# A table of steps in another order: blocks 2 to 8 of an attention and MoE kernel

## Chip, cores and metric

The kernel runs on one core of a Trainium2 chip. The metric is the time of one execution on the device in microseconds (us). Engines: PE multiplies matrices, DVE works on vectors, ACT on scalars and activations, POOL (GpSimd) issues most loads and stores here, SP issues the DMA transposes.

## What is computed

Eight batches (B), eight heads, 576 positions (S), head dimension 64. A linear attention without softmax is normed per head and position, and feeds a two-layer perceptron over 4608 tokens:

```python
kv = np.einsum('bhsd,bhse->bhde', k, v)
out = np.einsum('bhsd,bhde->bhse', q, kv)
rms = np.sqrt(np.mean(out * out, axis=-1, keepdims=True) + 1e-06)
x = (out / rms * g_norm).transpose(0, 2, 1, 3).reshape(4608, 512)
h = x @ w_in                                    # 512 -> 2048
g = np.maximum(h, 0.0) + alpha * np.minimum(h, 0.0)
y = g @ w_out                                   # 2048 -> 512, float32
```

## The kernel before

**Tiling.** The tokens are cut into nine blocks w = 0 to 8 of 512, each of four row tiles of 128. Blocks 0 and 1 are written out directly (the loop for block 1 is `loop_one`; its 16 units u take their PSUM banks h0, h1, h2 in turn, so that the last unit has h1). For blocks 2 to 8 the functions `put_m1`, `put_m2`, `put_moves`, `put_attention` and `put_rest` register *steps*, each with a name and the names that it needs. A string ORDER (L1856 on) lists all 1085 steps, and this generator emits them:

```python
def in_order():                                                     # L1960
    todo = {".".join(map(str, s[0])): s for s in steps if s[1]}
    names, done, gates = {s[0] for s in steps if s[1]}, set(), {"-": gt_last[0]}
    for x in ORDER:
        name, _, at = x.partition("@")
        s = todo.pop(name)
        assert all(n in done or n not in names for n in s[3]), name
        if at:
            load_gate[:] = [gates[at]] if at != "!" else []
        yield s[2]
        done.add(s[0])
        gates[name] = gt_last[0]
```

Each step's instructions go to the end of its engine's queue, and each engine works through its queue in order. So ORDER fixes for every engine what stands behind what; semaphores between engines follow from the data and from the tiles in PSUM and SBUF.

**The steps.** A name is a letter, the block, and numbers.

- First product, h = x w_in: `M.w.u` (L695, four matmuls 128x512; `M.w.0` and `Ma.w.0` split them into 128 and 384 columns, L728), `r.w.u` (ACT, relu of −h out of PSUM, L704), `s.w.u` (DVE, the PReLU sum into gt, L710). In blocks 3 to 8 twelve of the 16 units are instead made by three groups s = 1 to 3 of seven products (a Strassen-like scheme): `f.w.s.1` to `f.w.s.7` are eight or four 128x256 matmuls each (L1296), `seed`, `u2`, `u3` ACT copies (L1312, L1315), `c22`, `c12` DVE sums (L1318, tile mh), `r..` and `s..` the relu and PReLU sums (L1356, L1363). `t.` and `a.` are DVE sums of x and of weights.
- Second product, y = g w_out, by the same kind of scheme: `S.` are DVE sums of gt (L864 to L886), `p.w.n.k` groups of four 128x256 matmuls (L948), `y.w.seed`, `u2`, `u3` copies (L969, L996, L998), `y.w.c11`, `c21` (ACT, L1004) and `c12`, `c22` (DVE, L1010) the finished parts, `st.` their stores (L752).
- Attention: `ld.` are loads on POOL; with `@step` a one-element copy on POOL (L1478) that reads a result of that step holds the load back, `@!` is without such a gate. `q.b.t` is a DMA transpose of q by SP (L405), `kv.b` and `kvc.b` the product k^T v and its copies. `R.w.i` (i = 1 or 3) multiplies q with kv for two row tiles, i − 1 and i, in one tile or_ps over two PSUM banks, which the next R takes again (L575, 24 or 16 matmuls of 64x64). For each of the two row tiles follow `q2` and `q3` (ACT, four squares each with a sum, L635), `rs` (ACT, the reciprocal root, L645), `n` (DVE, the norm into x_rows, L661) and `x` (a DMA transpose by SP into xt, L673), which M and f of that block read. A *group* below is R with these steps; "group 3.2" or "at 8.3" names the pair of row tiles 2 and 3 of block 3 or 8.

The squares and the norm read the same tile or_ps for their own halves:

```python
nc.scalar.activation(                                               # L635, squares
    out=sq[:, half, j], in_=o_ps[:, half, j], func=AF.Square,
    accum_out=ssq[:, half, j : j + 1],
)
nc.vector.tensor_tensor(                                            # L661, norm
    out=xr[:].rearrange("p j h d -> p h j d"), in0=o_ps,
    in1=rstd[:].unsqueeze(3).to_broadcast([P, 2, NPAIR, D]), op=ALU.mult,
)
```

The first units M.w.0 to M.w.3 have fixed PSUM banks: u = 0 has h2, u = 1 has h1, u = 2 has m0, u = 3 has m1. The list of what a step needs names the steps of blocks 2 to 8 only; for the first use of a bank after `loop_one` it names nothing, and the semaphores alone hold the order there.

Of the kernel before, what the change touches and what calls it, by code (L numbers as in the profile page):

```python
# [17 lines left out]
def kernel(  # L18
# [13 lines left out]
    B, H, S, D = q.shape  # L32
# [1819 lines left out]
    for w in range(1, NW):  # L1852
# [4 lines left out]
        M.2.2 Ma.2.0 r.2.2 S.1.1.0 M.2.0 a.2.2 M.2.1 S.1.1.1 r.2.0 s.2.2 y.1.seed M.2.3 q.3.0  # L1857
        S.1.2.1 r.2.1 s.2.0 M.2.6 s.2.1 q.3.4 kv.3 S.1.1.2 S.1.2.0 p.1.2.3 a.1.3 q.3.1 kvc.3 M.2.4
        ld.k.4.1@- S.1.1.3 S.1.4.1 p.1.6.0 S.1.2.3 r.2.3 q.3.3 S.1.2.2 p.1.6.1 r.2.4 p.1.6.2 y.1.c11
        s.2.4 p.1.6.3 q.3.2 M.2.5 a.1.1 y.1.u2 s.2.3 p.1.7.0 r.2.5 M.2.7 ld.k.4.0@s.2.3 r.2.6 s.2.5  # L1860
        R.3.1 r.2.7 p.1.7.1 q2.3.1 ld.v.4.0@s.2.5 s.2.7 p.1.7.2 p.1.7.3 q2.3.0 s.2.6 M.2.8 S.2.3.0
        y.1.u3 ld.q.4.0@s.2.6 M.2.10 q3.3.0 ld.q.4.1@s.2.3 q3.3.1 M.2.9 ld.v.4.1@- rs.3.0 p.1.4.0
        rs.3.1 n.3.0 r.2.8 p.1.4.1 r.2.10 n.3.1 p.1.4.2 p.1.4.3 r.2.9 S.2.3.1 x.3.1 R.3.3 y.1.c21
        a.1.2 M.2.11 q2.3.2 a.1.4 s.2.8 x.3.0 p.1.5.0 q2.3.3 p.1.5.1 s.2.10 M.2.12 q3.3.2 s.2.9
        p.2.1.0 S.1.4.2 rs.3.2 p.1.5.2 q3.3.3 n.3.2 p.1.5.3 S.1.4.0 p.2.1.1 x.3.2 rs.3.3 r.2.11
        M.2.14 n.3.3 r.2.12 s.2.11 R.4.1 x.3.3 p.2.1.2 y.1.c22 q2.4.0 p.2.1.3 S.2.1.0 p.1.3.0 r.2.14
        q.4.2 M.2.13 y.2.p1 s.2.14 q2.4.1 p.2.2.0 S.1.4.3 q.4.0 s.2.12 M.2.15 q3.4.1 S.2.2.0 p.1.3.1
        q.4.3 r.2.15 p.2.2.1 q3.4.0 s.2.15 p.1.3.2 p.1.3.3 q.4.1 rs.4.1 ld.q.4.4@s.2.15 Ma.3.0
        rs.4.0 y.1.c12 r.2.13 M.3.0 n.4.0 ld.q.5.4@! M.3.2 r.3.0 s.2.13 y.2.seed x.4.0 M.3.3 r.3.2
        n.4.1 p.2.6.0 S.2.1.1 r.3.3 x.4.1 kv.4 s.3.0 M.3.1 t.3.1 kvc.4 ld.v.5.1@! S.2.2.1 f.3.1.1  # L1870
        s.3.2 r.3.1 p.2.6.1 t.3.2 p.2.6.2 f.3.1.seed st.1.c21 s.3.3 R.4.3 f.3.1.6 s.3.1 q2.4.3 q.5.4
        p.2.6.3 ld.q.5.0@s.3.0 t.3.3 f.3.1.2 f.3.1.u2 S.2.4.0 f.3.1.5 ld.q.5.1@s.3.2 y.2.u2 S.2.4.1
        f.3.1.7 f.3.1.r11 f.3.2.1 st.1.c11 t.3.4 f.3.1.u3 a.2.4 p.2.7.0 q2.4.2 f.3.1.c22 f.3.1.4
        p.2.7.1 f.3.1.s11 q3.4.3 f.3.1.3 p.2.7.2 f.3.1.r22 ld.v.5.0@! f.3.1.c12 p.2.7.3 rs.4.3
        p.2.2.2 f.3.2.seed n.4.3 p.2.2.3 y.2.u3 f.3.1.s22 f.3.2.6 x.4.3 f.3.1.r12 p.2.4.0 a.3.4
        f.3.2.u2 f.3.2.2 S.3.3.0 f.3.1.r21 f.3.2.7 f.3.1.s12 q3.4.2 p.2.4.1 f.3.2.5 f.3.1.s21
        f.3.2.u3 p.2.4.2 rs.4.2 p.2.4.3 f.3.2.r11 f.3.2.c22 f.3.3.1 y.2.c21 n.4.2 f.3.2.3 f.3.2.r22
        f.3.2.4 x.4.2 f.3.2.c12 y.2.c11 R.5.1 f.3.2.s22 p.2.5.0 f.3.3.seed p.2.5.1 f.3.2.r12 q.5.2
        f.3.2.s11 p.2.5.2 ld.k.5.0@f.3.2.s22 f.3.2.r21 f.3.3.6 f.3.2.s21 p.2.5.3 q.5.3 f.3.3.u2
# [124 lines left out]
```

## Time and profile before

| what | value |
|---|---|
| median of three runs | 271.4 us (270.56, 271.40, 271.46) |
| the profiled execution | 270.63 us |
| its span, first to last instruction | 268.8 us |
| ordered part (first M.2 to last matmul) | 66.6 to 264.7 us |
| busy PE / DVE / ACT | 259.5 / 234.4 / 201.8 us |

How to read it: the page gives the busy time of each engine and the chain of work that ended last. A row of the timeline has the start, the length, the engine, the line and operation, the tiles (out<-in), the shapes, how many instructions were joined (x4), and in brackets how long the engine had been idle before it and what released it. Matmuls are pipelined and their ends are modelled, so two rows of PE overlap; the time of a group is the distance from its start to the next start. "sq_sb" is the tile of the squares, "h_ps" that of M, "yX", "yY", "yZ" those of p, "mX", "mY", "mV" those of f.

### The profile page before, as it was taken

Reading aid. Unit: us, or ns where it says so; the run is one execution under the profiler, and the core shown is the slowest. Engines: PE = TensorE matmul, PEld = TensorE weight load, DVE = VectorE, ACT = ScalarE, POOL = GpSimd, SP = SyncE. Lnnn points to the kernel's source line nnn. Section 1 sums busy time; section 2 is a strip of 40 time slices with the busy share of each in tenths; the row PEclk is TensorE's granted clock in tenths of the full one; section 3 lists DMA queues with packets and bytes.
Section 4 is the critical chain, followed back from the end, with each engine's and each line's share of the span. In section 5 each row is a group of like instructions: output and inputs, shape, how many; then the busy total and the mean of one; then the engine's idle time right before and its main releaser. Section 6 shows DMA issues by size and latency. Waiting matters only on the chain.

```text
span 268.8 us, 7233 instructions
## 1 busy us (share of the span) xinstructions
PE 259.5 (97%) x2709; PEld 189.8 (71%) x2709; DVE 234.4 (87%) x474; ACT 201.8 (75%) x707; POOL 86.3 (32%) x150
## 2 busy tenths in 40 slices
PE   5999999999998999999999999999999989999993
PEld 2554454456565668887888688878886878788883
DVE  6459956899967889999999989999899899998982
ACT  2567637786688889988999799989998986568300
POOL 8853552554152039227012080520030005201400
PEclk9999999999999999999999999999999999999998
DMA  7999999998989899898968987998230314400423
GB/s 195 190 202 206 196 198 189 174 245 171 124 123 158 137 110 149 141 144 181 146 91 128 146 181 83 146 194 120 43 101 0 101 39 127 130 0 2 118 80 118
DMA packets 65032, 35.80 MB, mean 133 GB/s; under 512 B 37396, under 2 KB 63012, under 8 KB 64996
## 3 DMA queue, kind: packets, MB, share of 16 engines
q0 software_dynamic: 31792, 24.47, 58.9%
q1 hardware_dynamic: 32500, 10.11, 22.5%
q10 hardware_dynamic: 704, 0.75, 0.9%
q8 instruction: 21, 0.34, 0.5%
q14 instruction: 15, 0.12, 0.2%
HBM read 36.71 MB, written 9.44 MB: 172 GB/s over the span
## 4 chain that ended last, share of the span: by engine, by line
PE 85%; ACT 5%; DMA 4%; DVE 3%; issue 1%; SPq 1%; DVEq 0%
PE h_ps L695 19%; PE yY L948 13%; PE mY L1296 11%; PE yX L948 10%; PE yZ L948 9%; PE y L740 5%; PE mV L1296 5%; PE mX L1296 3%; ACT sq_sb L635 3%; DMA qt_sb<-qst 3%; PE h_ps L728 2%; PE or_ps L575 2%; DMA y_sb<-in_g_norm_dram 2%; PE kv_ps L1407 1%; PE ssq_ps L500 1%; ACT m_sb L1356 1%
## 5 line engine op out<-in xcount | busy, mean ns | idle before, releaser
L695 PE MATMUL h_ps<-xt,w_in_sb 128*128 128x512 f16 x252 | 60.4, 379 | 0.0
L710 DVE SCALAR_TENSOR_TENSOR gt<-m_sb,beta_sb,h_ps 128x512 f16<-128x512 f32 x72 | 51.8, 740 | 5.1 <-ACT m_sb L704 4.4
L704 ACT ACTIVATE m_sb<-h_ps 128x512 f32<-128x512 f32 x72 | 42.1, 604 | 15.6 <-PE h_ps L695 10.8
L948 PEld LDWEIGHTS <-s 128*128 128x128 f16 x496 | 47.7, 98 | 7.5 <-issue 0.2
L635 ACT ACTIVATE sq_sb<-or_ps 128x64 f16<-128x64 f32 x192 | 41.3, 271 | 2.7 <-PE or_ps L575 2.3
L948 PEld LDWEIGHTS <-gt 128*128 128x128 f16 x384 | 37.1, 98 | 7.8 <-issue 0.4
L695 PEld LDWEIGHTS <-w_in_sb 128*128 128x128 f16 x252 | 24.2, 98 | 23.2 <-issue 0.3
L635 ACT ACTIVATION_READ_ACCUMULATOR sq_sb<-or_ps 128x1 f32 x192 | 40.5, 256 | 0.0
L752 POOL DMA_DIRECT2D out_dram<-y_sb x37 | 21.5, 587 | 49.9 <-ACT y_sb L1004 43.6
L948 PE MATMUL yX<-w_out_sb,gt 128*128 128x256 f16 x256 | 36.6, 273 | 0.0
L948 PE MATMUL yY<-wsum,s 128*128 128x256 f16 x256 | 34.5, 273 | 0.0
L1363 DVE SCALAR_TENSOR_TENSOR gt<-m_sb,beta_sb,mh 128x256 f16<-128x256 f32 x72 | 31.1, 476 | 1.2 <-ACT m_sb L1356 1.2
L1356 ACT ACTIVATE m_sb<-mh 128x512 f32<-128x512 f32 x36 | 23.9, 664 | 3.0 <-DVE mh L1318 3.0
L1318 DVE TENSOR_TENSOR mh<-mV,mu 128x512 f32<-128x512 f32 x36 | 24.6, 684 | 1.5 <-PE mV L1296 0.8
L1315 ACT COPY mu<-mY 128x512 f32<-128x512 f32 x36 | 21.7, 602 | 3.7 <-PE mY L1296 3.6
L1296 PEld LDWEIGHTS <-w_in_sb 128*128 128x128 f16 x216 | 21.0, 98 | 3.6
L661 DVE TENSOR_TENSOR x_rows<-or_ps,rstd_r 128x512 f16<-128x512 f32 x27 | 18.1, 683 | 5.5 <-ACT sq_sb L635 2.7
L1478 POOL COPY gate_sb<-gt 1x1 f16<-1x1 f16 x17 | 5.4, 320 | 41.7 <-DVE gt L710 22.9
L948 PE MATMUL yY<-wsum,gt 128*128 128x256 f16 x128 | 16.7, 272 | 0.2 <-ACT u L996 0.2
L740 PE MATMUL y<-w_out_sb,gt 128*128 128x512 f16 x64 | 16.3, 380 | 0.0
L948 PE MATMUL yZ<-wsum,s 128*128 128x256 f16 x120 | 16.3, 273 | 0.0
L948 PE MATMUL yZ<-w_out_sb,s 128*128 128x256 f16 x120 | 16.2, 272 | 0.0
(161 smaller groups left out, 471.7 us busy)
## 6 DMA issues: line engine op xcount, KB each, us to landing
kst<-in_k_dram POOLq DMA_DIRECT2D x10, 288.0 KB, 5.3
vst<-in_v_dram POOLq DMA_DIRECT2D x10, 288.0 KB, 5.8
qst<-in_q_dram POOLq DMA_DIRECT2D x10, 256.0 KB, 5.7
out_dram<-y_sb POOLq DMA_DIRECT2D x18, 128.0 KB, 4.5
w_out_sb<-in_moe_w_out_dram POOLq DMA_DIRECT2D x8, 256.0 KB, 12.3
out_dram<-y_sb POOLq DMA_DIRECT2D x7, 256.0 KB, 4.0
out_dram<-y_sb SPq DMA_DIRECT2D x5, 256.0 KB, 2.4
w_in_sb<-in_moe_w_in_dram POOLq DMA_DIRECT2D x2, 512.0 KB, 10.0
```

What stands on the lines that cost most here:

```text
L635: nc.scalar.activation(out=sq[:, half, j], in_=o_ps[:, half, j], func=AF.Square, accum_out=ssq[:, half, j : j + 1],)
L695: nc.tensor.matmul(out=h_ps[:], lhsT=w_in_blk(c, g), rhs=xts[w][:, c, :], start=(c == 0), stop=(c == NC - 1),)
L704: nc.scalar.activation(out=neg[w, g][:], in_=h_ps[:], func=AF.Relu, scale=-1.0)
L710: nc.vector.scalar_tensor_tensor(out=gts[w, i][:, r, :], in0=neg.pop((w, g))[:], scalar=beta_sb[:, g : g + 1], in1=h_ps[:], op0=ALU.mult, ...
L740: nc.tensor.matmul(out=y[:], lhsT=gt_cols(w, g, a * P, (a + 1) * P), rhs=w_out_blk(g), start=(n == 1), stop=(n == NF),)
L752: engs[store_turn[0] % len(engs)].dma_start(out=dst, in_=src)
L948: nc.tensor.matmul(out=bank, lhsT=lhs, rhs=rhs, start=fresh, stop=(c == NK - 1), skip_group_check=True,)
L1296: nc.tensor.matmul(out=t[bank][:, r, :], lhsT=lhs[:, c, r * P : (r + 1) * P], rhs=rhs[:, c, :], start=(fresh and c == r == 0), stop=(c == ...
L1315: nc.scalar.copy(out=t[what][:], in_=t["Y"][:])
L1318: nc.vector.tensor_add(out=h_tile(t, what)[:], in0=src[:], in1=u[:])
L1356: nc.scalar.activation(out=dst, in_=h, func=AF.Relu, scale=-1.0)
L1363: nc.vector.scalar_tensor_tensor(out=gts[w, i][:, r, cols], in0=m, scalar=beta_sb[:, g : g + 1], in1=h, op0=ALU.mult, op1=ALU.add,)
```

## The change

The string ORDER is another permutation of the same 1085 steps (some loads have another gate); nothing else is changed. PE has the same 2709 matmuls. The difference has 99 lines of names on each side. These hold the first step and R.3.3, ahead of which the groups p.2.1.0 and p.2.1.1 now stand (before, they stood behind it):

```diff
-        M.2.2 Ma.2.0 r.2.2 S.1.1.0 M.2.0 a.2.2 M.2.1 S.1.1.1 r.2.0 s.2.2 y.1.seed M.2.3 q.3.0
...
-        rs.3.1 n.3.0 r.2.8 p.1.4.1 r.2.10 n.3.1 p.1.4.2 p.1.4.3 r.2.9 S.2.3.1 x.3.1 R.3.3 y.1.c21
...
-        p.2.1.0 S.1.4.2 rs.3.2 p.1.5.2 q3.3.3 n.3.2 p.1.5.3 S.1.4.0 p.2.1.1 x.3.2 rs.3.3 r.2.11
...
+        M.2.1 M.2.3 r.2.1 S.1.1.1 S.1.1.2 M.2.2 r.2.3 S.1.2.2 S.1.1.0 y.1.seed Ma.2.0 S.1.2.1
...
+        p.1.6.1 S.1.2.3 s.2.3 p.2.1.0 p.1.6.2 q.3.4 a.1.1 ld.v.4.0@s.2.3 M.2.4 S.1.4.3 s.2.2 M.2.5
...
+        p.1.4.3 R.3.3 s.2.9 y.1.c21 M.2.11 q2.3.2 x.3.0 s.2.10 p.1.5.0 q2.3.3 s.2.8 p.1.5.1 S.1.4.1
```

**PE where the ordered part begins.** The rows of PE from the last group of block 1 on; w_in_sb_166 and w_in_sb_157 are the weights of two units. Before, M.2.2 is first (bank m0) and Ma.2.0 next:

```order
L948 MATMUL yX<-w_out_sb_188,gt 128x256
L695 LDWEIGHTS w_in_sb_166 [waits DMAHW3_49,DMAHW2_49,DMAHW1_49]
L695 MATMUL h_ps<-xt,w_in_sb_166 128x512 [waits PE_49]
L695 LDWEIGHTS w_in_sb_166
L695 MATMUL h_ps<-xt,w_in_sb_166 128x512
```

Now, M.2.1 (bank h1) is first:

```order
L948 MATMUL yX<-w_out_sb_188,gt 128x256
L695 LDWEIGHTS w_in_sb_157 [waits DMAHW3_49,DMAHW2_49,DMAHW1_49]
L695 MATMUL h_ps<-xt,w_in_sb_157 128x512 [waits DVE_49]
L695 LDWEIGHTS w_in_sb_157
L695 MATMUL h_ps<-xt,w_in_sb_157 128x512
```

The first matmul waits for DVE now, before for PE's own earlier one.

**ACT at group 8.3.** or_ps is the group's tile. Before, its squares stand in four pieces of four; the rows from the second piece on, of which the last waits for DVE (the norm n.8.3):

```order
L635 ACTIVATE sq_sb,ssq_r<-or_ps 128x64 x4
L996 COPY u_4044<-yY 128x512 [waits PE_49]
L645 ACTIVATE rstd_r<-ssq_r,eps_t 128x8 [waits Activation_49]
L1356 ACTIVATE m_sb<-mh 128x512 [waits DVE_49]
L1312 COPY mX<-mY 128x512 [waits DVE_49]
L1356 ACTIVATE m_sb<-mY 128x512 [waits PE_49]
L635 ACTIVATE sq_sb,ssq_r<-or_ps 128x64 x4
L1315 COPY mu_4098<-mY 128x512 [waits PE_49]
L996 COPY u_4106<-yY 128x512 [waits PE_49]
L1356 ACTIVATE m_sb<-mh 128x512
L1315 COPY mu_4123<-mY 128x512 [waits PE_49]
L635 ACTIVATE sq_sb,ssq_r<-or_ps 128x64 [waits DVE_49]
```

Now they stand in two pieces of eight (the first is split in the list by its wait), all ahead of the group's first reciprocal root:

```order
L635 ACTIVATE sq_sb,ssq_r<-or_ps 128x64 [waits PE_49]
L635 ACTIVATE sq_sb,ssq_r<-or_ps 128x64 x7
L1315 COPY mu_4014<-mY 128x512 [waits PE_49]
L1356 ACTIVATE m_sb<-mX 128x512 [waits Activation_49]
L635 ACTIVATE sq_sb,ssq_r<-or_ps 128x64 x8
L996 COPY u_4060<-yY 128x512 [waits PE_49]
L645 ACTIVATE rstd_r<-ssq_r,eps_t 128x8 [waits Activation_49]
```

No square of this group waits for a norm any more, and copies stand behind eight squares instead of four.

**POOL around the q transposes of block 4.** Its queue of DMAs (L212, L229 loads of q, L202 of k and v, L752 stores). qsb_135 is ld.q.4.4, the four 64x256 pieces are st.1.c11, the 64x2x256 pieces st.1.c21. Before:

```order
L229 DMA qsb_135<-in_q_dram 64x8x64 [waits DMAHW5_49]
L229 DMA qsb_132<-in_q_dram 64x8x64 [waits DMAHW7_49,DMASW2_49]
L202 DMA vst<-in_v_dram 128x2x576 [waits DMASW3_49,DMASW0_49,PE_49]
L752 DMA out_dram<-y_sb 64x2x256 [waits DMASW4_49,Activation_49]
L752 DMA out_dram<-y_sb 64x2x256 [waits DMASW5_49]
L1478 COPY gate_sb<-gt 1x1 [waits DVE_49,Pool_49]
L212 DMA qst<-in_q_dram 128x4x256 [waits DMAHW2_49,DMAHW0_49,DMASW6_49]
L1478 COPY gate_sb<-gt 1x1 [waits DVE_49,Pool_49]
L212 DMA qst<-in_q_dram 128x4x256 [waits DMAHW7_49,DMAHW1_49,DMASW7_49]
L752 DMA out_dram<-y_sb 64x256
```

Now:

```order
L229 DMA qsb_135<-in_q_dram 64x8x64 [waits DMAHW5_49]
L752 DMA out_dram<-y_sb 64x256 [waits DMASW2_49,Activation_49]
L752 DMA out_dram<-y_sb 64x256 [waits DMASW3_49]
L752 DMA out_dram<-y_sb 64x256 [waits DMASW4_49]
L752 DMA out_dram<-y_sb 64x256 [waits DMASW5_49]
L1478 COPY gate_sb<-gt 1x1 [waits Pool_49]
L212 DMA qst<-in_q_dram 128x4x256 [waits DMAHW7_49,DMAHW0_49,DMASW6_49]
L1478 COPY gate_sb<-gt 1x1 [waits Pool_49]
L212 DMA qst<-in_q_dram 128x4x256 [waits DMAHW1_49,DMAHW2_49,DMASW7_49,DMASW0_49]
L229 DMA qsb_132<-in_q_dram 64x8x64
L752 DMA out_dram<-y_sb 64x2x256 [waits DMASW1_49,Activation_49]
```

The store st.1.c11 moved from behind the first loads of block 5 to directly behind ld.q.4.4, and the load of v.5.1 went out of this stretch.

More of the change, by code (lines that the diff above doesn't have):

```diff
@@ L1868 @@
[L1868 to L1879, printed above, removed]
@@ new lines @@
+        p.7.4.2 f.8.3.seed p.7.4.3 f.8.2.r12 f.8.2.s22 f.8.3.6 y.7.c21 f.8.3.2 f.8.2.s21 f.8.3.u2
+        p.7.5.0 f.8.3.r11 f.8.2.s12 p.7.5.1 p.8.1.1 f.8.3.s11 f.8.3.7 f.8.3.5 S.8.1.0 f.8.3.u3
+        p.7.5.2 f.8.3.c22 p.7.5.3 f.8.3.4 S.8.2.0 f.8.3.3 f.8.3.r21 y.7.c22 p.8.1.2 p.8.6.0
+        f.8.3.c12 st.7.c22 p.8.6.1 f.8.3.s21 f.8.3.r12 p.8.1.3 f.8.3.r22 p.7.3.0 f.8.3.s12 p.7.3.1
+        y.8.p1 st.7.c21 f.8.3.s22 p.7.3.2 p.8.2.0 p.8.2.1 S.8.1.1 p.8.2.2 S.8.2.1 p.8.2.3 p.7.3.3
+        y.8.c11 p.8.6.2 y.7.c12 p.8.6.3 p.8.5.0 st.7.c12 y.8.u2 p.8.5.1 S.8.4.0 p.8.7.0 p.8.7.1
```

174 lines of the change are left out of this document (90 added, 84 removed).

## The prediction, made before the changed kernel had run

> **What bounds the kernel now.** The page's first part and the slices come first: which engine is nearest to full, and is it slowed.
>
> ```profile
> span 268.8 us, 7233 instructions
> PE 259.5 (97%) x2709; PEld 189.8 (71%) x2709; DVE 234.4 (87%) x474; ACT 201.8 (75%) x707; POOL 86.3 (32%) x150
> PEclk9999999999999999999999999999999999999998
> ```
>
> PE's matmuls set the time, at nine tenths of the clock or more in every slice. The profiled execution took 270.63 us, so 1.8 us lie around its span. The change leaves all 2709 matmuls in place, so the sum is about PE's gaps. Next come the windows by stage; after each comma stand the busy times of PE, weight loads, DVE, ACT and POOL, then clock, DMA share and GB/s.
>
> ```profile
> 66.60:97.00 30.40, 29.27 (x314) 19.05 (x313) 24.09 (x46) 24.30 (x128) 7.64 (x18) 1.00 1.00 129
> 97.00:123.00 26.00, 26.00 (x315) 21.38 (x313) 25.43 (x53) 24.09 (x102) 11.70 (x19) 1.00 0.98 143
> 174.00:204.00 30.00, 29.82 (x356) 24.57 (x354) 29.05 (x61) 27.14 (x115) 4.73 (x8) 1.00 0.62 107
> 204.00:228.00 24.00, 23.20 (x215) 19.32 (x214) 22.92 (x47) 20.23 (x65) 3.15 (x6) 1.00 0.25 71
> ```
>
> From 97 to 123 us PE has no idle time, with DVE at 98% and ACT at 93% beside it. Nothing can be won in such a stage, and a late turn of DVE or ACT costs PE at once. The other three windows miss 1.13, 0.18 and 0.80 us. A matmul's end is modelled, so I measure gaps from start to start. The pitch comes from PE's timeline where it runs freely:
>
> ```profile
> 65.75 1.04 PE L948 MATMUL yX<-w_out_sb,gt 128*128 128x256 f16 x8
> 66.62 1.03 PE L695 MATMUL h_ps<-xt,w_in_sb 128*128 128x512 f16 x4
> 67.49 1.04 PE L728 MATMUL h_ps<-xt,w_in_sb 128*128 128x384 f16 x8
> ...
> 101.06 1.04 PE L948 MATMUL yY<-wsum,s 128*128 128x256 f16 x8
> 102.02 0.41 PE L575 MATMUL or_ps<-kv_masked,qt_sb 64*128 64x64 f16 x16
> ```
>
> Four 128x512 or eight 128x256 matmuls take 0.87 us, four of the latter 0.44. Ahead of a 64x64 group stand 0.96 − 0.87 = 0.09 us more, the same in both orders. In this way I went through all starts from 66.6 us on; four places are left:
>
> ```profile
> 83.15 0.29 PE L575 MATMUL or_ps<-kv_masked,qt_sb 64*128 64x64 f16 x8
> 84.42 0.29 PE L575 MATMUL or_ps<-kv_masked,qt_sb 64*128 64x64 f16 x8 [0.98 <-DMA qt_sb<-qst]
> 84.65 1.04 PE L695 MATMUL h_ps<-xt,w_in_sb 128*128 128x512 f16 x4
> ...
> 89.00 1.03 PE L695 MATMUL h_ps<-xt,w_in_sb 128*128 128x512 f16 x4
> 90.19 0.41 PE L575 MATMUL or_ps<-kv_masked,qt_sb 64*128 64x64 f16 x16 [0.15 <-DVE x_rows L661]
> ...
> 191.78 0.60 PE L1296 MATMUL mV<-xt,kst 128*128 128x256 f16 x4
> 192.56 1.03 PE L948 MATMUL yY<-wsum,gt 128*128 128x256 f16 x8 [0.18 <-ACT u L996]
> ...
> 216.59 1.04 PE L948 MATMUL yY<-wsum,gt 128*128 128x256 f16 x8
> 218.43 0.60 PE L1296 MATMUL mV<-xt,kst 128*128 128x256 f16 x4 [0.80 <-DVE mh L1318]
> ```
>
> In R.3.3 the first eight should take 84.65 − 84.42 = 0.23 us and took 1.27, a loss of **1.04**. R.4.1 could start at 89.00 + 0.87 + 0.09 and started at 90.19: **0.23**. The group p.5.4.0 is late by 192.56 − 192.22 = **0.34**, and f.7.2.3 by 218.43 − 217.46 = **0.97**. Together 2.58 us, the most that any order can win from these gaps: 268.05.
>
> **The change part by part: what goes.** Three of the four come from the exclusion. The squares (ACT) and the norms (DVE) of a group's two row tiles touch one PSUM tile, and the queues show one waiting for the other:
>
> ```profile
> 87.36 0.30 ACT L645 ACTIVATE rstd_r<-ssq_r,eps_t 128x8 f32<-128x8 f32 x1
> 88.16 0.23 ACT L635 ACTIVATE sq_sb<-or_ps 128x64 f16<-128x64 f32 x1
> 191.10 0.22 ACT L635 ACTIVATE sq_sb<-or_ps 128x64 f16<-128x64 f32 x1 [0.31 <-DVE x_rows L661]
> 191.91 0.60 ACT L996 COPY u<-yY 128x512 f32<-128x512 f32 x1
> 212.04 0.30 ACT L645 ACTIVATE rstd_r<-ssq_r,eps_t 128x8 f32<-128x8 f32 x1
> 214.35 0.25 ACT L635 ACTIVATE sq_sb<-or_ps 128x64 f16<-128x64 f32 x1
> ```
>
> ```profile
> 88.51 0.69 DVE L661 TENSOR_TENSOR x_rows<-or_ps,rstd_r 128x512 f16<-128x512 f32 x1 [1.89 <-ACT sq_sb L635]
> 89.45 0.68 DVE L661 TENSOR_TENSOR x_rows<-or_ps,rstd_r 128x512 f16<-128x512 f32 x1
> 190.38 0.68 DVE L661 TENSOR_TENSOR x_rows<-or_ps,rstd_r 128x512 f16<-128x512 f32 x1
> 214.72 0.69 DVE L661 TENSOR_TENSOR x_rows<-or_ps,rstd_r 128x512 f16<-128x512 f32 x1 [0.84 <-ACT sq_sb L635]
> 217.69 0.69 DVE L1318 TENSOR_TENSOR mh<-mV,mu 128x512 f32<-128x512 f32 x1
> ```
>
> At 3.2 the scale was there at 87.66, yet n.3.2 began at 88.51, just behind the other tile's squares; n.3.3 then ended at 90.13, and R.4.1 took the banks at 90.19. At 7.3 the squares had to let n.7.2 pass (end 191.06), and the copy that p.5.4.0 needs stood behind them. At 8.3 the scale was ready at 212.34, n.8.3 waited for squares until 214.6, and DVE, full from there on, brought mh only at 218.38. In the new order all sixteen squares of 3.2 and 8.3 stand ahead of the first norm, and n.7.2 stands where the next copy is not held. R.4.1 gets at most 0.35 us of slack, p.5.4.0 its 0.34. At f.7.2.3 the 0.84 us of waiting leaves 0.13 us open if nothing else moved; the new order puts that norm behind other work, so I take the whole 0.97 and keep 0.13 among the small terms. Similar crossings stay at 4.2, 5.2 and 6.3, where before shows no gap.
>
> The fourth gap, R.3.3, is a transpose of q:
>
> ```profile
> 75.04 3.82 SPq L405 DMA_TRANSPOSE qt_sb<-qst  x3
> 91.83 6.02 SPq L405 DMA_TRANSPOSE qt_sb<-qst  x4
> ```
>
> ```profile
> 77.61 6.77 DMA qt_sb<-qst
> ```
>
> ```profile
> DMA to landing us min/median/max: 2.4/4.9/6.8
> L405 SPq DMA_TRANSPOSE qt_sb<-qst x20: 1189/1236/2172, 69.9 to 184.1; - x20
> ```
>
> The last of the three before it was issued at 77.61 and landed at 84.38. SP's queue is the same up to there. The new order puts p.2.1.0 and p.2.1.1, two groups of 0.44, ahead of R.3.3, and the late start below adds 0.77: R.3.3 begins at 83.15 + 0.87 + 0.77 = 84.8. The stall goes, 1.04 us.
>
> **What is added.** The ordered part now begins with M.2.1, whose first matmul waits for DVE; before, M.2.2 began it. The bank belonged to the last unit of block 1, and DVE reads it in this row:
>
> ```profile
> 66.58 0.75 DVE L710 SCALAR_TENSOR_TENSOR gt<-m_sb,beta_sb,h_ps 128x512 f16<-128x512 f32 x1 [0.39 <-ACT m_sb L704]
> ```
>
> It ends at 67.33; DVE to PE took 0.06 above (90.13 to 90.19). So PE starts at 67.39 and not at 66.62: **+0.77**. All later matmuls queue behind it, and with no idle stretch on PE nothing absorbs it but the stalls that it shortens (R.3.3's is already counted once). DVE and ACT lose no work through it, so their chains get up to 0.77 us of lead; I credit nothing for that, with 0 to −0.3 as bounds.
>
> **The q transposes of block 4.** R.4.3 started at 102.02 without a wait. Its last transpose was issued at 91.83 + 6.02 − 1.24 = 96.6, so by the median landing it was there at 101.5: half a microsecond of slack. In the new order R.4.3 comes at 102.02 + 0.87 (two more groups ahead) + 0.77 − 1.04 − 0.23 = 102.4. The transposes hang on x.3.3, some 0.6 us later; I take the last issue at 97.2. It lands at 99.6 by the shortest, 102.1 by the median, 104.0 by the longest time. That is a stall of 0 to 1.6 us; between median and longest I take **0.3**. What makes it likelier than before: the store st.1.c11 and the load ld.q.4.4 now stand on POOL's queue in the window of these transposes.
>
> The Trainium skill, page "Trainium Kernel Development and Optimization", section Key Constraints, says that DMAs issued from SP, ACT and POOL share the same 16 DMA engines and interleave. By that rule the moved store slows SP's transposes and this term would be nearer 1.6 us, the sum below nearer 270.9; if separate queues kept out of each other's way, the term would be 0 and the sum 269.3. The trace agrees in so far as one form of transfer took between 2.4 and 6.8 us.
>
> **Small terms.** Both orders hold some twenty places where a result goes from PE through a copy (0.60 us, the row at 191.91) back to PE with two groups (0.87 us) or fewer between. Counted by PE's work between them they are 23 before and 20 now, but they are other ones. One missed turn costs what the four gaps above cost, 0.23 to 0.97. At f.5.3.6 I find 0.11, in the last stage (the c12 result of block 7 now stands three groups ahead of p.8.5.0, before five) 0.1, at f.7.2.3 up to 0.13; for one unseen missed turn 0.2. Together **0.5**, between 0 and 1.5.
>
> **The sum.** 270.63 − 2.58 + 0.77 + 0.3 + 0.5 = 269.6 on the profiled run's scale, where the bounds of the terms give 268.5 (268.05 + 0.77 − 0.3) to 271.9 (268.05 + 0.77 + 1.6 + 1.5). That run lies 0.77 under the median of 271.4, and the runs fall near 270.6 or near 271.4; I add half of that and forecast **270.0**.
>
> **The rivals.**
> (a) The gain is eaten: the start costs 0.77, the transposes 1.0, one or two missed turns 0.8. 268.05 + 2.6 = 270.6, or 271.4 by the median: no change. For it: DVE at 98% and ACT at 93% in the full window. Against: the four gaps have causes that the order takes away.
> (b) The order keeps what it takes: 268.05 + 0.77 = 268.8, with half the offset 269.2. For it: the crossings that cost PE are gone. Against: R.4.3's slack of nearly nothing.
> (c) **Slower:** ACT's squares in one piece.
>
> ```profile
> 191.10 0.93 ACT sq_sb L635 x8
> ```
>
> In this chain row four squares with their reads take 0.93 us. The new order has 16 squares in a row at group 3.2, 12 at 8.1 and 8 twice at 8.3, behind which copies and scales stand that PE needs. Four squares more ahead of a copy cost PE 0.93 us from the point where the copy had less than that to spare. Four or five such places make 3.7 to 4.7: 269.6 + 3.7 to 269.6 + 4.7, or 273 to 274. For it: ACT has two microseconds to spare in 26. Against: the copies that I followed around these runs still arrive within their groups.
> (d) The change does not do what it says: only three of the six crossings go. Where those left cost PE something now, (a) comes of it; I give it no time of its own.
>
> **How the numbers follow.** The forecast has 0.36 (269.4 to 270.6), (a) with (d) 0.24 (270.6 to 271.8), (b) 0.14 (268.6 to 269.4), (c) 0.26 (from 272.8). A measurement of this kernel tells about 0.5% from no change, 1.36 us: faster is under 270.04, slower over 272.76. Of the forecast 0.22 lies below 270.04 and 0.14 above: faster 0.22 + 0.14 = 0.36, same 0.14 + 0.24 = 0.38, slower 0.26. The range is 268.6 to 273.0, which leaves out the upper half of (c) and a little of (b). The likeliest case's own range is 269.4 to 270.6.
>
> **What the profile after would show.** The first M.2 group waits for DVE and starts 0.7 to 0.8 us later against the end of block 1. R.3.3 runs as sixteen without a DMA wait, R.4.1 without one for x_rows. No norm waits for squares at 3.2 and 8.3. R.4.3 shows a DMA wait of 0 to 1.6 us on qt_sb. A wait of more than a microsecond of PE for a copy behind a run of squares would speak for (c), and gaps at places that before ran freely for (a). If PE's total idle time falls by more than 1.5 us, (b) holds. The forecast is wrong if R.3.3 still waits, or if the start costs nothing.

## The result and the profile after

The new order takes 268.61 us in the median of six runs (268.16 to 269.63), the order before 271.43 (270.56 to 275.73 in six): a ratio of 0.9895 with a 95% interval of 0.9851 to 0.9939, **faster by 2.8 us**, about 1%. The forecast was 270.0; its rival (b), which had 268.6 to 269.4 and a chance of 0.14, is what came, at the lower edge of its interval. The profiled execution took 268.16 us, 2.47 less than the one of before.

The page's head and the windows at the four stages shown of before:

```profile
span 266.4 us, 7239 instructions
PE 259.3 (97%) x2709; PEld 190.0 (71%) x2709; DVE 234.3 (88%) x474; ACT 201.3 (76%) x707; POOL 85.7 (32%) x152
```

```profile
66.60:97.00 30.40, 29.76 (x317) 19.37 (x316) 25.24 (x50) 24.74 (x129) 9.76 (x22) 1.00 1.06 132
97.00:123.00 26.00, 26.00 (x314) 21.32 (x313) 24.43 (x51) 23.86 (x100) 8.37 (x17) 1.00 1.05 142
...
174.00:204.00 30.00, 30.00 (x353) 24.14 (x350) 28.89 (x60) 27.45 (x108) 3.81 (x6) 1.00 0.60 123
204.00:228.00 24.00, 24.00 (x229) 20.62 (x228) 23.88 (x51) 19.43 (x65) 4.52 (x8) 1.00 0.28 78
```

The work is the same (259.3 against 259.5 us on PE); from 97 to 228 us PE is now never idle. Only the first window still misses 0.64 us. PE's timeline shows where, and the places of the four gaps:

```profile
65.59 1.04 PE L948 MATMUL yX<-w_out_sb,gt 128*128 128x256 f16 x8
67.22 2.10 PE L695 MATMUL h_ps<-xt,w_in_sb 128*128 128x512 f16 x9 [0.59 <-DVE gt L710]
...
84.68 0.41 PE L575 MATMUL or_ps<-kv_masked,qt_sb 64*128 64x64 f16 x16
...
91.20 0.41 PE L575 MATMUL or_ps<-kv_masked,qt_sb 64*128 64x64 f16 x16
...
102.16 0.41 PE L575 MATMUL or_ps<-kv_masked,qt_sb 64*128 64x64 f16 x16
...
191.87 1.91 PE L948 MATMUL yY<-wsum,gt 128*128 128x256 f16 x16
...
216.31 0.60 PE L1296 MATMUL mV<-xt,kst 128*128 128x256 f16 x4
```

The ordered part starts 67.22 − (65.59 + 0.87) = 0.76 us late, for the last PReLU sum of block 1, as forecast. R.3.3 runs as sixteen without a wait for its transposes; R.4.1, R.4.3, p.5.4.0 (191.87) and f.7.2.3 (216.31) carry no bracket. No new gap has come.

To sum it up I split each profiled execution into the head (to the end of block 1's last group), the ordered part (from there to the end of the last matmul) and the tail, and took every start distance on PE beyond the pitch, over all matmuls of the ordered part:

| | before | after | difference |
|---|---|---|---|
| head | 66.62 | 66.46 | −0.16 |
| start wait | 0 | 0.76 | +0.76 |
| distances beyond the pitch | 7.63 | 4.94 | −2.69 |
| tail, last matmul to end of span | 4.12 | 3.78 | −0.34 |
| around the span | 1.79 | 1.77 | −0.02 |

They add up to −2.45 of the 2.47 us. On PE the start wait and the distances together fall by 1.93 us, more than the 1.5 us that the prediction set as the sign of (b). Of the −2.69 the four gaps are 2.58, R.3.3 gives 0.12 back (it now waits for the norms of group 3.0 and starts at 84.68, not 84.56), and small distances have gone for 0.23. Behind R.3.3 no start in the new order is more than 0.15 us beyond the pitch. The shorter tail belongs to the order too: it is 4.0 to 4.1 us in the profiles of before and of its five edited versions, and 3.4 to 3.9 us in all eleven of the new order and its versions.

### The profile page after: what moved, and what is told of

Same layout as the page of the kernel before. It is cut to its first block, busy times and chain, and to the rows that moved or that the text cites. A ratio compares the mean times of both kernels' runs of the same rounds, so it can differ in the third digit from the quotient of the medians.

```text
span 266.4 us, 7239 instructions
## 1 busy us (share of the span) xinstructions
PE 259.3 (97%) x2709; PEld 190.0 (71%) x2709; DVE 234.3 (88%) x474; ACT 201.3 (76%) x707; POOL 85.7 (32%) x152
## 4 chain that ended last, share of the span: by engine, by line
PE 93%; ACT 3%; DMA 1%; DVE 1%; SPq 1%; issue 0%; ACTq 0%
PE h_ps L695 20%; PE yY L948 15%; PE mY L1296 12%; PE yX L948 10%; PE yZ L948 10%; PE mV L1296 6%; PE y L740 5%; PE mX L1296 3%; PE h_ps L728 2%; PE or_ps L575 2%; DMA y_sb<-in_g_norm_dram 1%; PE kv_ps L1407 1%; ACT sq_sb L635 1%; PE ssq_ps L500 1%; PE ot_ps L477 1%; ACT m_sb L704 1%
## 5 line engine op out<-in xcount | busy, mean ns | idle before, releaser
L752 POOL DMA_DIRECT2D out_dram<-y_sb x37 | 21.5, 587 | 47.9 <-ACT y_sb L1004 37.2
L1478 POOL COPY gate_sb<-gt 1x1 f16<-1x1 f16 x19 | 4.4, 232 | 45.9 <-DVE gt L1363 23.1
L948 PE MATMUL yZ<-wsum,s 128*128 128x256 f16 x120 | 17.1, 273 | 0.0
L948 PE MATMUL yY<-wsum,gt 128*128 128x256 f16 x128 | 16.1, 272 | 0.0
```

Source lines behind the costliest of these rows:

```text
L752: engs[store_turn[0] % len(engs)].dma_start(out=dst, in_=src)
L948: nc.tensor.matmul(out=bank, lhsT=lhs, rhs=rhs, start=fresh, stop=(c == NK - 1), skip_group_check=True,)
```

## The experiments

Each ran beside the order before on the same chip, whose medians there were 271.57, 271.85, 272.1, 271.86 and 271.25. Times vary by a few tenths to some microseconds between executions of one kernel, and the head, which no edit but one touches, ended between 66.5 and 68.0 in these profiles. So an edit of under a microsecond is judged by the ordered part of its profile, named "ordered" below: 198.10 before, 196.15 after. That is one execution each, and waits for DMAs differ between executions.

**The new order again**, as control.

> The new order itself, on the same chip and beside the same runs of the order before as the kernels sent with it. Expected 2.5 to 3 us less than before, as in the first result. In its profile R.3.3 is the place to look at: if its start wait is a real price of 0.76 us, R.3.3 shows no DMA wait; if the transposes are late in this execution, R.3.3 waits in spite of the later start.

268.56 us, ratio 0.9897 (0.9857 to 0.9937); ordered 196.27, start wait 0.76, no DMA wait at R.3.3.

### Group 8.3: is it the exclusion?

**Only the direction turned round** (in before):

```diff
- f.7.2.6 q2.8.2 n.8.3 p.6.7.2
+ f.7.2.6 n.8.3 q2.8.2 p.6.7.2
```

> The old order with the names n.8.3 and q2.8.2 exchanged: every engine's queue stays as it was, only the direction of the exclusion between the norm of row tile 3 and the first squares of row tile 2 turns round. Theory (the exclusion made DVE late, and that made f.7.2.3 late): DVE does not wait at n.8.3, which starts at 213.9 instead of 214.7, mh comes 0.84 us earlier, and the gap at f.7.2.3 falls from 0.97 to about 0.13; ACT waits about 0.8 us ahead of q2.8.2 instead, and if a copy behind it is needed soon, a gap of up to 0.8 us appears there. Time 0.8 us less than before, or the same if ACT's wait costs it again. Rival (DVE is full there and mh would be late anyway): gap at f.7.2.3 stays within 0.2 us of 0.97.

270.84 us, ratio 0.9988 (0.9958 to 1.0018), ordered 197.75. ACT, then PE:

```profile
215.81 0.22 ACT L635 ACTIVATE sq_sb<-or_ps 128x64 f16<-128x64 f32 x1 [0.65 <-DVE x_rows L661]
```

```profile
216.13 0.60 PE L1296 MATMUL mV<-t,kst 128*128 128x256 f16 x4
217.26 0.60 PE L1296 MATMUL mY<-t,kst 128*128 128x256 f16 x4 [0.53 <-ACT mu L1315]
```

No queue changed, yet now ACT waits for the norm, the gap at f.7.2.3 is gone, and f.7.2.7 is late by 217.26 − (216.13 + 0.44) = 0.69 for the copy behind those squares. So the exclusion is the cause, and it only chose which engine pays: 0.97 became 0.69.

**The squares in one piece, as the new order has them** (in before):

```diff
- q3.8.3 ... rs.8.3 ... q2.8.2 n.8.3 ... q3.8.2
+ q2.8.2 q3.8.3 q3.8.2 ... rs.8.3 ... n.8.3
```

> The order before with the squares of group 8.3 as the new order has them: q2.8.2 directly ahead of q3.8.3 and q3.8.2 behind it, all sixteen ahead of the group's first reciprocal root; nothing else. Theory: no norm and no square waits for the other, f.7.2.3 loses its 0.97 us and f.7.2.7 does not get the 0.69 that turning the direction round gave it: 0.8 to 1.0 us less than before. Rival (ACT's squares in one piece hold up the copies behind them): the u and mu copies behind the twelve squares come up to 1.6 us later and PE waits there for as much as was won.

271.91 us, ratio 1.0006 (0.9972 to 1.0039), ordered 199.69. The rival holds:

```profile
212.93 0.60 PE L1296 MATMUL mY<-t,w_in_sb 128*128 128x256 f16 x4
214.86 1.03 PE L948 MATMUL yY<-wsum,s 128*128 128x256 f16 x8 [1.33 <-ACT u L996]
```

```profile
214.10 0.72 ACT L996 COPY u<-yY 128x512 f32<-128x512 f32 x1
```

Twelve squares stand ahead of the copy u; p.6.7.0 is 1.49 us late, f.7.2.3 no longer. (Of the 1.59 us that ordered is above before, 0.89 are a longer wait of R.3.3 for transposes, which this edit doesn't touch.) That is the mechanism of my slower rival (c), real in the old surroundings. The new order has none of this gap: its squares stand in two pieces of eight with a copy between, and p.6.2.2 ahead of p.6.7.0; which of the two avoids it was not tested.

**The old crossing put back into the new order:**

```diff
- st.4.c12 q2.8.2 S.6.1.1 ... p.6.6.1 q3.8.2 p.6.6.2 ... f.7.2.6 f.7.1.s22 ... n.8.3 f.7.2.u3 p.6.2.3
+ st.4.c12 S.6.1.1 ... p.6.6.1 p.6.6.2 ... f.7.2.6 q2.8.2 n.8.3 f.7.1.s22 ... f.7.2.u3 q3.8.2 p.6.2.3
```

> The new order with the crossing of before put back at group 8.3 alone: q2.8.2 behind f.7.2.6, n.8.3 directly behind it, q3.8.2 behind f.7.2.u3, so that n.8.3 waits for squares and q3.8.2 for n.8.3. Theory: DVE waits at n.8.3 and what stands behind it comes late, as before: a gap of 0.5 to 1 us on PE between f.7.2.7 and f.7.2.3, and as much more time than the new order. Rival: the new order has its slack at 8.3 from other moves, the wait of DVE stays without effect on PE, and the time is within 0.2 us of the new order.

269.98 us, ratio 0.9952 (0.9918 to 0.9986), ordered 197.13: 0.98 more than the new order.

```profile
214.62 0.69 DVE L661 TENSOR_TENSOR x_rows<-or_ps,rstd_r 128x512 f16<-128x512 f32 x1 [0.84 <-ACT sq_sb L635]
```

```profile
215.11 0.60 PE L1296 MATMUL mY<-t,kst 128*128 128x256 f16 x4 [0.19 <-ACT mu L1315]
...
218.88 1.36 PE L948 MATMUL yY<-wsum,gt 128*128 128x256 f16 x11 [0.31 <-ACT u L996]
```

The wait of DVE is back to the hundredth (0.84), and PE pays in three pieces (0.36, 0.24 and 0.47 beyond the pitch). The theory holds in the new order too.

### All four gaps by local edits

```diff
- p.1.4.3 r.2.9 S.2.3.1 x.3.1 R.3.3      ...  R.4.1 x.3.3 p.2.1.2
+ p.1.4.3 ... p.2.1.0 p.2.1.1 R.3.3      ...  x.3.3 p.2.1.2 R.4.1
- n.7.2 p.5.7.3 q3.7.3 ... y.5.u3        ...  q2.8.2 n.8.3
+ n.7.2 p.5.7.3 y.5.u3 q3.7.3            ...  n.8.3 q2.8.2
```

> The old order with four local edits, one for each gap: p.2.1.0 and p.2.1.1 ahead of R.3.3; R.4.1 behind p.2.1.2; y.5.u3 ahead of q3.7.3; n.8.3 ahead of q2.8.2. Theory (the whole gain is these four gaps): R.3.3 loses 0.87 of its 1.04 (0.17 left), R.4.1 0.23, p.5.4.0 0.34, f.7.2.3 0.84 or more; together 2.2 to 2.6 us less than before, 268.0 to 268.4 on the scale of the profiled run of before, with the start at once. Rival (a full machine: what is taken away at one place is late at the next): new gaps at the places behind, total gain under 1.2 us.

271.23 us, ratio 0.9993 (0.9963 to 1.0022), ordered 198.36: nothing won. The theory that the gain is four separate gaps falls; "taken away here, late at the next place" holds:

```profile
84.85 0.29 PE L575 MATMUL or_ps<-kv_masked,qt_sb 64*128 64x64 f16 x8 [0.41 <-DMA qt_sb<-qst]
...
90.62 0.41 PE L575 MATMUL or_ps<-kv_masked,qt_sb 64*128 64x64 f16 x16 [0.59 <-DVE x_rows L661]
...
91.87 0.60 PE L948 MATMUL yZ<-w_out_sb,s 128*128 128x256 f16 x4 [0.30 <-DVE y_sb L1010]
...
216.51 0.60 PE L1296 MATMUL mY<-t,kst 128*128 128x256 f16 x4 [0.53 <-ACT mu L1315]
```

The two groups ahead of R.3.3 are now missing between R.3.3 and R.4.1, and R.4.1 waits longer (0.59 in the bracket, 0.15 before) though it stands one group later. At p.5.4.0 the gap went, and f.6.3.6 two places on is late by 0.29.

### The start wait and the transposes of block 3

**M.2.2 first in the new order.**

```diff
- M.2.1 M.2.3 r.2.1 S.1.1.1 S.1.1.2 M.2.2
+ M.2.2 M.2.1 M.2.3 r.2.1 S.1.1.1 S.1.1.2
```

> The new order with one step moved: M.2.2 (bank m0) ahead of M.2.1 (bank h1), nothing else. Theory: the 0.76 us by which the new order starts its ordered part late is only the wait of M.2.1 for the last PReLU sum of block 1; with M.2.2 ahead (0.87 us of PE work) PE starts at once and M.2.1 finds the bank free. Expected 0.7 to 0.8 us less than the new order: 267.4 on its profiled run's scale, the first M group directly behind the last group of block 1. Rival: the late start was a lead that DVE and ACT use, so that the gap comes back at R.3.1, R.3.3 or R.4.1 and the time stays within 0.2 us of the new order.

268.76 us (267.73 to 271.06), ratio 0.9915 (0.9886 to 0.9944): no gain in the median. In its profile PE starts at once, and then:

```profile
86.08 0.23 PE L575 MATMUL or_ps<-kv_masked,qt_sb 64*128 64x64 f16 x4 [1.60 <-DMA qt_sb<-qst]
```

R.3.3 waits for its transposes again. This execution is the slowest of the seven (271.06 us), so its wait is not that of the median run; that the median gains nothing says only that the 0.76 us are lost again somewhere in most of them.

**The same late start in the order before.**

```diff
- M.2.2 Ma.2.0 r.2.2 S.1.1.0 M.2.0 a.2.2 M.2.1
+ M.2.1 M.2.2 Ma.2.0 r.2.2 S.1.1.0 M.2.0 a.2.2
```

> The order before with M.2.1 moved ahead of M.2.2, so that its ordered part begins with the same wait of 0.76 us as the new order's; nothing else. Theory (the late start has no price of its own, since R.3.3 waits for transposes of q whose time does not hang on PE): R.3.3's wait, 0.98 us in the profile of before, shrinks by about 0.76, and the time stays within 0.3 us of before. Rival (what the prediction summed): 0.76 us is added to the end, the median is 0.6 to 0.9 us above that of before.

271.26 us, ratio 0.9993 (0.9966 to 1.002), ordered 198.34: 0.24 more than before, not 0.76.

```profile
67.45 1.89 PE L695 MATMUL h_ps<-xt,w_in_sb 128*128 128x512 f16 x8 [0.59 <-DVE gt L710]
...
75.10 1.05 PE L948 MATMUL yY<-wsum,s 128*128 128x256 f16 x8 [0.39 <-DVE s L882]
...
84.51 0.41 PE L575 MATMUL or_ps<-kv_masked,qt_sb 64*128 64x64 f16 x16
...
90.52 0.41 PE L575 MATMUL or_ps<-kv_masked,qt_sb 64*128 64x64 f16 x16 [0.28 <-DVE x_rows L661]
```

The start wait took the place of R.3.3's wait; new are 75.10 − (73.67 + 0.87) = 0.56 us at p.1.6.2, whose sums now come late (the group ahead of it began at 73.67), and 0.13 more at R.4.1. All six profiles that begin with M.2.1 (the new order, a_ctrl, a_dma, a_cross83, a_sq5, b_start) show no DMA wait at R.3.3; the five that begin at once with SP's queue as before (before, b_flip83, b_merge83, b_four, a_start) show 0.98, 0.72, 1.87, 0.41 and 1.60. The theory holds in its time: here the late start is nearly free.

Its reason was too simple: the time of the transposes seems to hang on PE after all. With the start at once the last one that R.3.3 needs landed at 84.4 to 86.0 in these profiles; with the late start at 79.6 to 81.8, as far as the landings are recorded, which is 2.9 to 5.0 us ahead of R.3.3 and not 0.76. One thing that the late start moves there is a load of k for block 4 on POOL, which here waits for the product kv.3 on PE. POOL and SP in before, then in b_start (the row with qsb is q.3.4; the three transposes behind it start at 75.04 in before, as the prediction shows):

```profile
72.15 0.71 POOL L202 DMA_DIRECT2D kst<-in_k_dram  x1 [4.45 <-PE kv_ps L1407]
73.77 1.17 SPq L405 DMA_TRANSPOSE qt_sb<-qsb  x1
```

```profile
72.98 0.70 POOL L202 DMA_DIRECT2D kst<-in_k_dram  x1 [5.20 <-PE kv_ps L1407]
72.39 1.35 SPq L405 DMA_TRANSPOSE qt_sb<-qsb  x1
73.84 3.82 SPq L405 DMA_TRANSPOSE qt_sb<-qst  x3
```

In before this load was issued while the load that q.3.4 needs was still under way (it landed at 73.62); in b_start that one had landed, at 72.24. So q.3.4 was issued 1.4 us earlier, the three behind it 1.2 us earlier, and the last two, now further ahead of the next loads, took 3.9 and 3.2 us to land instead of 6.5 and 6.8. That the load of k is the cause was not tested by moving it alone.

**The transposes sooner.** Four tries to have both. The first puts q.3.4 behind the others, in before and in the new order (there with M.2.2 first; only SP's transposes of block 3 are shown, in the new order's sequence):

```diff
- q.3.0 q.3.4 q.3.1 q.3.2 q.3.3
+ q.3.0 q.3.1 q.3.2 q.3.3 q.3.4
```

> The order before with q.3.4 alone moved behind q.3.2. Theory: R.3.3's wait of 0.98 us for qt_sb goes, and R.4.1 follows it by the same chain of squares and norms of 5.7 us, so that its gap stays near 0.3: 0.9 to 1.0 us less than before. Rival: what R.3.3 no longer waits, R.4.1 or R.4.3 wait instead, and the time stays within 0.3 us of before.

> The new order with M.2.2 ahead of M.2.1, and SP's transpose q.3.4 (the remainder of batch 3, not needed by R.3.3) moved behind the four transposes that R.3.3 needs. Theory: with the earlier start alone R.3.3 waited 1.60 us for a transpose of q, since q.3.4 held SP's queue until its own load was there (74.19) and the other three stood behind it. Now they are issued from about 71.3 on, the last at about 75, and land by 82; R.3.3 at about 83.9 runs free, so the whole 0.76 us is won: 0.6 to 0.9 us less than the new order. Rival: landing takes 6 to 7 us however early the issue, or the norms of group 3.0 are late instead, and the gain is under 0.3 us.

271.47 us (ratio 0.9981, 0.9942 to 1.002) and 271.2 us (0.996, 0.992 to 1.0): both theories miss. The first has its rival's time, but not for the rival's reason; the second is slower than the new order by more than two microseconds. I had read q.3.4 as not needed by then. R.3.1 needs it; PE in b_q34, then in a_best (executions of 273.14 and 274.03 us, slower than their medians):

```profile
80.50 0.54 PE L575 MATMUL or_ps<-kv_masked,qt_sb 64*64 64x64 f16 x16 [2.35 <-DMA qt_sb<-qsb]
```

```profile
82.96 0.75 PE L575 MATMUL or_ps<-kv_masked,qt_sb 64*64 64x64 f16 x16 [3.49 <-DMA qt_sb<-qsb]
```

The second, with M.2.2 first, lets only q.3.1 pass q.3.4:

```diff
- q.3.0 q.3.4 q.3.1 q.3.2 q.3.3
+ q.3.0 q.3.1 q.3.4 q.3.2 q.3.3
```

> The new order with M.2.2 ahead of M.2.1 and q.3.1 ahead of q.3.4 on SP. The runs before showed that R.3.1 needs q.3.4 (it waited 3.49 us when q.3.4 stood last), so it can't stand behind all four; but while q.3.4 waits for its load, q.3.1 can go. Theory: the last transpose that R.3.3 needs is issued up to 1.2 us earlier, and R.3.3's wait, 1.60 us in the profile with M.2.2 first, falls by that; the median falls 0.3 to 0.7 us below the new order. Rival: q.3.1's own load lands no earlier than that of q.3.4 (in two runs q.3.1's issue took 2.1 and 2.8 us in that place), R.3.1 then waits for q.3.4, and the time is that of the new order or up to 1 us more.

268.54 us (267.54 to 269.54), ratio 0.9899 (0.9854 to 0.9944): the median of the new order. R.3.3 ran free after a start at once, but kv.7 came late, and ordered is 196.15 again:

```profile
177.60 0.77 PE L1407 MATMUL kv_ps<-vst,kst 64*64 64x64 f16 x72 [0.55 <-ACT m_sb L1356]
```

ACT is named, but had long been done; a load of k for this product landed at 176.69, and I took that for the cause. So the third also issued this load sooner:

```diff
- ld.v.7.0@! ... ld.k.7.0@f.5.2.s11
+ ld.k.7.0@! ld.v.7.0@!
```

> The new order with M.2.2 ahead of M.2.1, q.3.1 ahead of q.3.4, and the load ld.k.7.0 without its gate and ahead of ld.v.7.0. With the first two alone the ordered part had R.3.3 free and began at once, but kv.7 waited 0.55 us (its load of k landed at 176.69, just before it), and the median stayed that of the new order. Theory: with that load about 2 us earlier nothing on PE waits for a DMA in the ordered part, it takes 195.4 to 195.6 us instead of 196.2, and the median is 0.5 to 0.8 us below the new order's 268.6. Rival: another transfer is late instead and the median stays within 0.3 us of 268.6.

269.04 us, ratio 0.9892 (0.9858 to 0.9925), ordered 197.34; kv.7 waited longer:

```profile
179.05 0.77 PE L1407 MATMUL kv_ps<-vst,kst 64*64 64x64 f16 x72 [1.74 <-ACT m_sb L1356]
```

The cause was another. kv.7 takes a bank that the norms of group 7.0 read, and it begins when the second of these ends. DVE in a_q134, then in a_best3:

```profile
172.89 0.42 DVE L1280 TENSOR_TENSOR t<-xt 128x512 f16<-128x512 f16 x1 [0.61 <-DMA xt<-x_rows]
...
176.22 1.28 DVE L661 TENSOR_TENSOR x_rows<-or_ps,rstd_r 128x512 f16<-128x512 f32 x2
```

```profile
174.34 0.42 DVE L1280 TENSOR_TENSOR t<-xt 128x512 f16<-128x512 f16 x1 [1.91 <-DMA xt<-x_rows]
...
177.66 1.29 DVE L661 TENSOR_TENSOR x_rows<-or_ps,rstd_r 128x512 f16<-128x512 f32 x2
```

A sum of x waits for the transpose x.6.3, and DVE's whole queue with the norms behind it. That transpose took 4.78 us to land in the new order (5.11 in a_ctrl), 6.25 in a_q134, 7.54 in a_best3, where both loads stand right beside it. In a_q134 they stand as in the new order, and why it took longer there stays open. The fourth moves both loads ahead of it:

```diff
- x.6.1 ... ld.v.7.0@! ... ld.k.7.0@f.5.2.s11
+ x.6.1 ld.k.7.0@! ld.v.7.0@!
```

> The new order with M.2.2 ahead of M.2.1, q.3.1 ahead of q.3.4, and the loads ld.k.7.0 and ld.v.7.0 moved forward to directly behind x.6.1, without the other gate. This mends a misreading of the two runs before: kv.7 was late not for its load but for the norms of group 7.0 (n.7.0 ended at 177.50, kv.7 began at 177.60; 178.95 and 179.05 in the other), which stood on DVE behind a sum that waited 0.61 and 1.91 us for the transpose x.6.3; that transpose took 6.25 and 7.54 us to land, against 4.78 in the new order, with these two loads issued beside it. Theory: with the loads some 4 us earlier x.6.3 lands in under 5 us, DVE does not wait, kv.7 comes on time, the ordered part takes 195.3 to 195.6 us and the median is 0.5 to 0.8 us below 268.6. Rival: the loads then meet x.6.1 or x.6.2, or x.6.3 takes as long whatever stands beside it, and the median stays within 0.3 us of 268.6 or above.

271.21 us, ratio 0.9991 (0.996 to 1.0022), ordered 197.29. The rival holds: the loads met x.6.2, issued 0.5 us after the second of them. It landed in 6.63 us, where it took 2.39 to 2.41 in the four profiles without a load beside it (the new order, a_ctrl, a_q134, a_best3); x.6.3 took 7.28, and kv.7 is late by 0.92. Another 0.82 us is lost at 171.02, where PE waits for a copy of ACT that waited 1.35 us for a store. So the 0.76 us was not won in any of these tries: each time a transfer became late instead.

**The loads of q for block 3 sooner.** M.2.2 first, and the gate of the three loads two units earlier in block 1:

```diff
- LOADS = {(1, 1): (("k", 3), ("v", 3)), (1, 13): (("q", 3),)}
+ LOADS = {(1, 1): (("k", 3), ("v", 3)), (1, 11): (("q", 3),)}
```

> The new order with M.2.2 ahead of M.2.1, and the three loads of q for batch 3 gated two units earlier in block 1 (on POOL they then follow the stores directly, at about 61.4 instead of 64.7). Theory: the start wait of 0.76 us has no price only because R.3.3 would otherwise wait for transposes of q, whose chain begins with these loads; with the loads 3.3 us earlier the transposes end before R.3.1 and R.3.3 need them, both start without a DMA wait, and the 0.76 us are won: median 267.6 to 268.0, below that of the new order alone by 0.6 to 0.9. Rival: the loads collide with the stores and loads ahead of them and land no earlier, or another chain (the norms of group 3.0) is late at R.3.3; then the median stays within 0.3 us of the new order.

274.4 us, ratio 1.0125 (1.0085 to 1.0164), the one clear loss:

```profile
72.39 4.33 PE L695 MATMUL h_ps<-xt,w_in_sb 128*128 128x512 f16 x12 [4.30 <-DMA xt<-x_rows]
```

The transposes of q did land by 78.7, before they were needed; but the three loads were issued beside the transposes of x for block 2, and the last of these took 7.6 us to land instead of 2.5. The very first M waited 4.30 us for it.

### The slack at R.4.3 and on ACT

**A store more in the window of the q.4 transposes.**

```diff
- st.1.c11 q2.4.0 ... st.1.c21 t.3.2
+ st.1.c11 st.1.c21 q2.4.0 ... t.3.2
```

> The new order with the store st.1.c21 (256 KB) moved from 101.5 to directly behind st.1.c11, into the window of the q transposes of block 4 (92 to 98). Theory of the prediction (R.4.3 has next to no slack, and stores in that window slow the transposes): the transposes take 6 to 7 us to land instead of 4 to 5 and R.4.3 waits 0.5 to 2 us for qt_sb. Rival (slack of two or more microseconds): R.4.3 runs without a DMA wait.

268.18 us in its one run, R.4.3 at 102.16 without a wait as in the new order: the rival holds, there is slack. The last transposes were issued at 94.8 and 96.9 and the last landed at 100.0, more than two microseconds ahead.

**One square more in each of the steps q2 and q3 of blocks 4 to 8** (a repeat of the first; the result is the same):

```diff
-         for j in range(NPAIR):
+         for j in [0] * (w > 3) + list(range(NPAIR)):
```

> The new order with one more square (a repeat of the first) in every q2 and q3 step of blocks 4 to 8: 40 more squares of 0.195 us from start to start, 7.8 us more of ACT's time, the result unchanged. Theory of the prediction (ACT at 93% in the middle window, nothing to spare, every late turn costs PE at once): PE loses 4 to 7.8 us. Rival: the busy time counts rows whose ends overlap the next row's start (a copy is 0.60 us long but 0.48 us from start to start), ACT has about a fifth of its time free, and PE loses less than 1.5 us.

278.09 us; ordered 206.32, 10.2 more than the new order for 7.8 us of squares. From 97 to 123 us:

```profile
97.00:123.00 26.00, 24.45 (x295) 19.48 (x294) 22.62 (x46) 25.16 (x113) 7.74 (x15) 1.00 1.11 114
```

PE has 1.55 us of idle time there and had none. So the prediction's reading holds against the rival: the stage has no slack on ACT.

## Why the forecast was too small

**The four gaps** were read rightly: 2.58 us, gone but for 0.12. My reasons for their going were not all right. At 8.3 the exclusion is the cause (b_flip83, a_cross83). At R.3.3 I let two groups and the late start cover a landing at 84.38; the transposes landed at about 81.8, so this gap went as forecast, but by luck as to the reason. At 7.3 the copy stood behind the squares: put ahead of them (b_four) it closed that gap. In the new order it still stands behind four of them, but n.7.2 is ahead of them all and two more groups (p.6.1.0, f.6.3.1) are ahead of p.5.4.0; which of these counts was not tested. At 3.2 I named the norm that waits for squares. The new order takes this wait away, but the chain is no shorter. DVE, new order:

```profile
88.78 0.68 DVE L661 TENSOR_TENSOR x_rows<-or_ps,rstd_r 128x512 f16<-128x512 f32 x1
...
90.04 0.68 DVE L661 TENSOR_TENSOR x_rows<-or_ps,rstd_r 128x512 f16<-128x512 f32 x1
```

From the last eight matmuls of R.3.3 to the end of the second norm it was 90.13 − 84.42 = 5.7 us before and is 90.72 − 84.80 = 5.9 now. R.4.1's gap went because one more group, M.2.15 with 0.87 us, stands between R.3.3 and R.4.1; in b_four, with one group of 0.44 us fewer than before, it grew.

**The start**: +0.77 forecast, 0.76 measured. But the two terms are one thing: I took 1.04 for R.3.3 and added 0.77 for the start, and without the late start R.3.3 would still wait (a_start). Their sum, −0.27, came out near it, at −0.16; read as a price that an edit could win back, 0.77 was wrong.

**The step that failed is what I put on top**: "between median and longest I take **0.3**" at R.4.3 and "Together **0.5**" for small terms. R.4.3 measured 0, with more than two microseconds of slack in a_dma. The profile of before was a poor guide to that slack: there the last of its transposes took 5.23 us and landed at 101.82, only 0.20 us ahead of R.4.3, but in four edited versions of before it was 1.5 to 2.8 us ahead, and in a_dma, a_q134 and a_sq5 2.2 to 3.1. The small terms measured −0.23 on PE, and the last stage, +0.1 in the forecast, −0.34 by the tail. With 0 in place of 0.8 the sum on the profiled run's scale is 268.8; from there to 268.16 it is mostly the tail (−0.34), the small distances (−0.23) and the head (−0.16, which the order doesn't touch), less the 0.12 at R.3.3. I charged the new order for missed turns that I had not found in it, only because its chains are tight: they are (a_sq5 costs more than the work added), but all arrive in time. By half the offset between run and median I added 0.39; the median of after lies 0.45 over its profiled run, so that term came out.

**The rule of the shared DMA engines** (the Trainium skill, "Trainium Kernel Development and Optimization", Key Constraints) I weighed at the wrong place. At R.4.3 moved stores cost nothing. The runs agree with it at other places: in a_load, with loads on POOL's queue beside it, a transpose on SP's took 7.6 us instead of 2.5, and in a_best4 two loads beside x.6.2 took its landing from 2.4 to 6.6 us.

**Rival (c)** had a real mechanism (b_merge83: 1.49 us), but in the new order no place shows it.

**No version beat the new order** clearly: a_start and a_q134 have the lowest single runs (267.73 and 267.54), but medians within 0.2 us of it. What stays open is whether some place for the loads of block 7 suits an earlier start: two places were tried, and both slowed a transpose of x.

## What to carry to other kernels

Where one engine is full and two others nearly so, a gap is not a place but a ring of waits: closing it alone moves it (b_four won nothing, 99 reordered lines won 2.8 us), so price such a reordering from the gaps that the new order really has; a lump for gaps that were not found was the error here. When two engines read one PSUM tile and exclude each other, turning the order of the names round only chose who waits here; the new order, with the squares ahead of the norm and other work between, had no gap. And before a late start is counted as a cost, look for the next DMA wait behind it, and for the transfers that it holds back, since it may pay for itself there.

## Of the hardware, not expected

After R.3.3's wait of 1.60 us in the profiled execution of a_start, the granted clock fell to half for 3.4 us (86.9 to 90.3); in the windows (PE, weight loads, DVE, ACT, POOL, clock, DMA share, GB/s):

```profile
84.00:86.00 2.00, 0.43 (x13) 0.26 (x12) 1.84 (x3) 0.70 (x2) 0.00 (x0) 1.00 1.29 177
86.00:88.00 2.00, 1.92 (x11) 1.03 (x12) 1.16 (x3) 1.64 (x17) 0.77 (x1) 0.71 1.35 198
88.00:90.00 2.00, 2.00 (x12) 1.44 (x10) 0.00 (x0) 2.00 (x20) 0.00 (x0) 0.50 1.36 187
90.00:94.00 4.00, 4.00 (x25) 2.29 (x23) 3.26 (x6) 2.39 (x5) 0.00 (x0) 0.97 0.34 52
```

A 128x256 matmul took 0.213 us from start to start there and not 0.109, so the wait cost about twice its length: ordered is 198.93 in that profile, 3.5 us more than the new order's 196.15 without its start wait. After 3.49 us (a_best) and 4.30 us (a_load) the clock fell too, each time for 3.4 us; after 1.87 (b_merge83) and 2.35 us (b_q34) the pitch stayed whole. The Trainium skill, page "TensorE: Matmul & The Clock Gate", section "What's actually happening", has the half rate after an idle window of about 3.4 us, and a window that runs freely. The free running agrees with a fall after one wait and none after a longer one. That 1.60 us of waiting, next to R.3.3's short matmuls, came before a fall differs from that length, and the measurement decides; it is one execution, and that the wait caused the fall is read from their order in time alone.
